# Attention: row sums turned into rows by TensorE, and scores as three products of float32r parts

## The chip, the cores and the metric

The kernel runs on one core of a Trainium2 chip. The metric is the device time of one execution in microseconds (us). Three runs of the kernel before took 1138.47, 1144.91 and 1147.83 us; the median is 1144.91. A profile of one execution, with every instruction's start, duration and waits, is what the prediction is made from.

## The reference, cut to what matters

The whole reference is attention over 4 batches of 8 heads, a gated feed-forward layer that mixes positions, and a layer of 8 experts with one expert per token. The change touches the attention alone:

```python
# q, k, v: (4, 8, 1152, 64) float32
q_pool = q.reshape(B, H, S // 2, 2, D).mean(axis=3)          # 576 queries a head
scores = (1 / sqrt(D)) * matmul(q_pool, k.transpose(0, 1, 3, 2))   # 576 x 1152
scores = scores - max(scores, axis=-1, keepdims=True)
attn = exp(scores)
attn = attn / (sum(attn, axis=-1, keepdims=True) + 1e-09)
return matmul(attn, v)
```

## The kernel before

The 32 heads are handled as 16 pairs (`NP`). A head has 576 queries: four blocks of 128 and a last 64. A pair therefore has nine tiles of 128 queries (`NTL = 9`), listed in `KIND`: eight are one block of one head, the ninth (`t == 8`, `KIND` None) holds the last 64 queries of both heads. There are 144 tiles, numbered g.

For one tile:

- `scores`: queries times the 1152 keys, contraction over 64 values. The keys lie in two halves of the partitions: rows 0 to 63 hold keys 0 to 511 and then 1024 to 1151, rows 64 to 127 hold keys 512 to 1023. The queries stand in both halves. So keys 0 to 1023 are two f32 matmuls of 512 columns, one per row half, into two banks of `s`. In tile 8 each head fills one half of the output's partitions, so there are four matmuls, one per quadrant of the array. An f32 matmul is two instructions in the profile.
- `scores_rest`: the last 128 keys, from rows 0 to 63 alone, into the bank `r` (128 of its 512 columns).
- `maximum`: VectorE takes the minimum over `s`, then over `r` (the queries are scaled by -1/16, so the minimum is the maximum of the scores).
- `exps`: ScalarE's exponentials into `e`, with their sums into `sum`.
- `transp`: TensorE transposes `e` in two parts, five and four blocks of 128 keys, each block in two row halves (10 and 8 instructions), into `t`, of which there is one buffer. `back` copies `t` to `et` in SBUF: the first part on VectorE (L149), the second on ScalarE (L147).

A pair's tiles 0 to 3 form its first half (c = 0) and tiles 4 to 8 its second (c = 1). Per half:

- `sums`: VectorE adds the two sums of each tile and takes reciprocals (`rs`: one partition per query, one column per tile). Then SP stores them to `rdram` in DRAM as rows: L164 twice, and for c = 1 L167 twice. `spread` reads them back, each row broadcast to 64 partitions, as `rb` (L175, for c = 1 also L177).
- `push`: AV, the product of `v` and `et`, nine blocks of keys per head, cut into steps of 2, 2, 2 and 3 blocks, one step per tile. The result stands in the one bank `av`. `out` (L198, L200) multiplies it by `rb` into `xo` and frees the bank; SP writes `xo` to `xT` (L201), which the next stage reads.

The order is written by hand: each function is put at a time in tiles (`at(g + .2, scores_rest, g)`), and the list, sorted by time, is the order on every engine's queue. Scores of tile g stand at g, the first transposes of tile g at g + 1.98, the copy L149 at g + 2.1, the second transposes at g + 2.15, an AV step at g + 0.5, an AV half's scaling at g + 1.11 behind its last step. The sums of tiles 3 and 8 stand at g + 2.13 and the spread at g + 5.05. SP, which issues all these transfers, works through its queue in order and waits where an entry is not ready.

The next pair's queries and keys are loaded at tiles 0 and 1 (`load_qk`), one head each; `prep` adds neighbouring queries and scales them (L71, L72), on GpSimd at tiles 3 and 4; for the first pair VectorE does it ahead of everything. Beside this, steps of a later stage's weight conversion (`bg`, L295 to L354) run on VectorE, ScalarE and GpSimd in tiles 0, 1, 2, 6, 7 and 8 of each pair.

## Time and profile before

| | before |
|---|---|
| median of 3 runs | 1144.91 us |
| profiled execution | 1142.15 us |
| its span on the core | 1140.4 us |
| mean granted TensorE clock | 0.954 of full |
| TensorE busy | 1017.6 us (89%) |
| VectorE busy | 743.2 us (65%) |
| ScalarE busy | 595.6 us (52%) |
| GpSimd busy | 229.1 us (20%) |

The span runs from the first to the last instruction of the program; the rest of the profiled execution's time lies around it. A busy share is a mean over stages with different limits: attention fills the span up to about 592 us, the feed-forward layer the next part and the experts the last. PE is TensorE's matmuls and PEld its weight loads, DVE VectorE, ACT ScalarE, POOL GpSimd, and SPq the queue of SyncE, which issues DMAs. Matmuls overlap, so the duration of one is longer than the distance at which the next one starts.

### The profile page before, as it was taken

The numbers are of one execution on the slowest core, as the hardware profiler recorded it, in microseconds if no ns is written. First come the engines' busy times: TensorE is split into PE (matmuls) and PEld (weight loads), VectorE is DVE, ScalarE is ACT, GpSimd is POOL, SyncE is SP. The second block draws the span as 40 slices with busy tenths as digits, with TensorE's granted clock in tenths as the row PEclk, the third lists the DMA queues.
The fourth block names the chain that finished last, engine by engine and source line by source line (L and its number), as shares of the span: only waits on it lengthen the run. The fifth ranks groups of instructions, "written<-read, shape, count | busy, mean of one in ns | idle before, by whom it ended". The sixth has DMA issues, their size and how long they took to land.

```text
span 1140.4 us, 19804 instructions
## 1 busy us (share of the span) xinstructions
PE 1017.6 (89%) x7500; PEld 685.5 (60%) x7500; DVE 743.2 (65%) x1329; ACT 595.6 (52%) x1172; POOL 229.1 (20%) x189
## 2 busy tenths in 40 slices
PE   6679878799989969989947999999999999999997
PEld 3234434344444434444436898899777777777775
DVE  5558766577876757766718861423378877888784
ACT  4346645466656646655614332212237767776773
POOL 1001110111110111110025341122121413133221
PEclk9789988999999989989978899999999999999999
DMA  5346745456756756737153211200283314111750
GB/s 153 85 84 103 113 90 124 70 114 113 109 117 126 88 95 121 94 105 144 36 151 111 66 53 39 75 1 1 91 285 143 120 47 176 37 38 50 279 222 26
DMA packets 68128, 116.78 MB, mean 102 GB/s; under 512 B 30858, under 2 KB 39218, under 8 KB 66488
## 3 DMA queue, kind: packets, MB, share of 16 engines
q1 hardware_dynamic: 64304, 104.38, 39.4%
q0 software_dynamic: 3680, 11.02, 2.9%
q8 instruction: 63, 1.03, 0.5%
q14 instruction: 41, 0.34, 0.2%
q10 hardware_dynamic: 40, 0.01, 0.0%
HBM read 165.61 MB, written 19.48 MB: 162 GB/s over the span
## 4 chain that ended last, share of the span: by engine, by line
PE 44%; issue 20%; DMA 19%; DVE 10%; POOL 3%; ACT 2%; SPq 2%; another core or an unknown queue 0%; POOLq 0%; DVEq 0%; ACTq 0%
PE ps_av L190 10%; PE ps_t L131 8%; DMA aw_rb<-rdram 7%; DMA rdram<-aw_rs 6%; PE ps_s L82 5%; DMA er_x<-x,tab_gi 4%; PE m_ps_v L608 4%; PE m_ps_u L556 4%; PE m_ps_u L542 3%; PE m_ps_v L501 3%; POOL er_x L983 2%; PE ps_r L95 2%; DVE aw_et L149 2%; DVE aw_mx L105 2%; PE ps_s L85 1%
## 5 line engine op out<-in xcount | busy, mean ns | idle before, releaser
L131 PEld LDWEIGHTS ps_t<-keep_ident,aw_e 64*128 64x128 f32 x2592 | 107.6, 143 | 225.8 <-DVE aw_et L149 145.0
L190 PE MATMUL ps_av<-aw_et,aw_v 128*64 128x320 f32 (+1 forms) x1152 | 175.3, 433 | 38.2 <-DVE aw_xo L200 38.2
L105 DVE TENSOR_REDUCE aw_mx<-ps_s 128x1 f32<-128x1024 f32 x144 | 174.8, 1214 | 15.4 <-PE ps_s L82 8.4
L131 PE MATMUL ps_t<-keep_ident,aw_e 64*128 64x64 f32 x2592 | 146.3, 239 | 42.8 <-DVE aw_et L149 32.7
L149 DVE COPY aw_et<-ps_t 128x640 f32<-128x640 f32 x144 | 118.7, 824 | 95.4 <-PE ps_t L131 84.3
L119 ACT ACTIVATE aw_e<-ps_s,aw_mx 128x1024 f32<-128x1024 f32 x144 | 159.2, 1105 | 0.0
L82 PE MATMUL ps_s<-ao_k,ao_q 64*128 64x512 f32 x512 | 148.2, 659 | 7.3 <-DMA ao_k<-in_k 5.9
L117 ACT ACTIVATE aw_e<-ps_r,aw_mx 128x128 f32<-128x128 f32 x144 | 52.9, 368 | 163.8 <-DVE aw_junk L106 163.2
L190 PEld LDWEIGHTS ps_av<-aw_et,aw_v 128*64 128x64 f32 x1152 | 74.3, 142 | 89.8 <-DVE aw_xo L200 39.5
L147 ACT ACTIVATE aw_et<-ps_t 128x512 f32<-128x512 f32 x144 | 86.0, 597 | 77.2 <-PE ps_t L131 70.5
L354 DVE TENSOR_TENSOR eb_w2l<-er_r,eb_w2h 128x1024 fp32r<-128x1024 f32 x88 | 103.5, 1218 | 4.6 <-ACT eb_w2h L350 4.4
L354 DVE TENSOR_TENSOR eb_w1l<-er_r,eb_w1h 128x1024 fp32r<-128x1024 f32 x66 | 78.8, 1221 | 34.1 <-ACT eb_w1h L350 34.1
L350 ACT ACTIVATE eb_w2h<-er_r 128x1024 fp32r<-128x1024 f32 x88 | 88.7, 1068 | 0.6 <-PE ep_yp L1056 0.3
L71 POOL TENSOR_TENSOR ao_qr<-ao_qr 128x576 f32<-128x576 f32 x30 | 42.4, 1414 | 213.5 <-DMA ao_qr<-in_q 181.2
L350 ACT ACTIVATE eb_w1h<-er_r 128x1024 fp32r<-128x1024 f32 x66 | 67.8, 1072 | 18.1 <-DMA er_r<-in_w 8.5
L1056 PE MATMUL ep_yp<-eb_w2h,ew_hth 128*128 128x512 f32 x176 | 71.1, 404 | 0.3 <-ACT ew_hth L350 0.3
L1056 PE MATMUL ep_yp<-eb_w2h,ew_htl 128*128 128x512 f32 x176 | 70.2, 399 | 0.2 <-DVE ew_htl L354 0.2
L1056 PE MATMUL ep_yp<-eb_w2l,ew_hth 128*128 128x512 f32 x176 | 69.1, 393 | 0.0
L1062 POOL DMA_INDIRECT out<-ew_y,tab_si x22 | 22.4, 1017 | 202.6 <-DVE ew_y L1061 176.7
L106 DVE TENSOR_SCALAR_CACHE_REDUCE aw_junk<-ps_r,aw_mx 128x128 f32<-128x128 f32 x144 | 50.6, 351 | 19.1 <-PE ps_r L95 0.6
L501 PE MATMUL m_ps_v<-keep_wv,m_a_xh 128*128 128x512 f32 x144 | 47.0, 400 | 14.7 <-issue 13.7
L354 POOL TENSOR_TENSOR bg_l<-bg_e,bg_h 128x256 fp32r<-128x256 f32 x16 | 11.6, 727 | 237.7 <-ACT bg_h L350 237.7
(234 smaller groups left out, 1905.0 us busy)
## 6 DMA issues: line engine op xcount, KB each, us to landing
er_r<-in_w SPq DMA_DIRECT2D x45, 2048.0 KB
ao_qr<-in_q SPq DMA_DIRECT2D x32, 576.0 KB
ao_k<-in_k SPq DMA_DIRECT2D x32, 320.0 KB
aw_v<-in_v SPq DMA_DIRECT2D x16, 576.0 KB
xT<-aw_xo SPq DMA_DIRECT2D x16, 288.0 KB
bg_raw<-in_w_in SPq DMA_DIRECT2D x16, 256.0 KB
aw_rb<-rdram SPq DMA_DIRECT2D x64, 64.0 KB
er_r<-in_w SPq DMA_DIRECT2D x16, 256.0 KB
```

What stands on the lines that cost most here:

```text
L82: nc.tensor.matmul(d["s"][:, i, :], r["q", h][rows, 128 * n:128 * n + 128], r["k", h][rows, 0:512], start=True, stop=True)
L105: nc.vector.tensor_reduce(out=m[:, 0:1], in_=d["s"], op=ALU.min, axis=AX.XY)
L117: nc.scalar.activation(out=e[:, 8, :], in_=d["r"][:, 0:128], func=AF.Exp, bias=d["m"][:, 1:2], scale=-1.0, accum_out=s[:, col, 1:2])
L119: nc.scalar.activation(out=e[:, 0:8, :].rearrange("p k c -> p (k c)"), in_=d["s"].rearrange("p i c -> p (i c)"), func=AF.Exp, bias=d["m"][ ...
L131: nc.tensor.transpose(t[:, i, 64 * (k - k0):64 * (k - k0) + 64], E[g]["e"][o, k, :], ident[o, o])
L147: nc.scalar.activation(out=o, in_=i, func=AF.Copy)
L149: nc.vector.tensor_copy(o, i)
L190: nc.tensor.matmul(box["t"][64 * h:64 * h + 64, 0:n], v[:, h, k, :], et[:, k, h, 0:n], start=k == 0, stop=k == 8)
L350: nc.scalar.activation(out=hi, in_=src, func=AF.Copy)
L354: (nc.gpsimd if eng_lo == "p" else nc.vector).tensor_tensor(out=lo, in0=src, in1=hi.bitcast(F32), op=ALU.subtract)
L501: nc.tensor.matmul(pv, xx[xi][:, k, tile(i, j)], wv[:, wj, k, :], start=n == 0, stop=n == 11)
L1056: nc.tensor.matmul(pt, hT[hi][:, c, 128 * o:128 * o + 128], W2[wi][:, f, :], start=f == 0 and (hi, wi) == (0, 0), stop=f == 7 and (hi, wi) ...
```

## The change

It has three parts.

**Sums.** The stores L164 and L167 are gone. `sums_turn`, at g + 2.25, transposes the columns of `rs` on TensorE into columns 128 to 255 of the bank `r` of tile g + 2, on 4 or 5 partitions. `maximum` of that tile copies these rows to SBUF on VectorE between its two minima, and SP stores them to `rdram` as rows. `spread` moves from g + 5.05 to g + 4.05 and reads two rows per head, and for c = 1 half a row more. The last pair's second half has no later tile, so `sums_last` takes a bank of its own.

**Scores.** Queries and keys are split into two float32r parts, hi and lo. The scores are hi hi + hi lo + lo hi, three products per row half that add up in one bank. Tile 8 no longer uses quadrants: the last 64 queries of head 0 stand in columns 512 to 575 and those of head 1 in columns 576 to 639, with zeros for the other head's, and both heads' three products add up over all 128 rows of the output: six per row half. The rest of the scores is three (tile 8: six) float32r products of 128 columns.

**Splitting.** GpSimd has six instructions per head instead of two, on 640 columns instead of 576, in tiles 2 to 7, two at a time. For the first pair (`head`) VectorE and ScalarE do it. Keys now pass through a raw buffer `kr`, of which there is one per head. Queries are loaded with 640 columns.

```diff
@@ -43,66 +43,95 @@
-        E, ET, SUM, MX, TP = {}, {}, {}, {}, {}
+        E, ET, SUM, RS, TP = {}, {}, {}, {}, {}
...
+        QW = 640
...
         def load_qk(p, h):
...
-                r["qr", h] = opr([128, 2, SQ], F32, f"qr{h}", bufs=1)
+                r["qr", h] = opr([128, 2, QW], F32, f"qr{h}", bufs=1)
...
-                r["k", h] = opr([128, 640], F32, f"k{h}")
-                nc.sync.dma_start(r["k", h], ap["k"][p, h])
+                r["kr", h] = opr([128, 640], F32, f"kr{h}", bufs=1)
+                nc.sync.dma_start(r["kr", h], ap["k"][p, h])
...
         def load_v(p):
...
-        def prep(p, h, e, o=0, n=SQ):
+        def parts(p, h):
+            r = P[p]
+            r["q", h] = [opr([128, QW], F32R, f"q{i}{h}") for i in "hl"]
+            r["k", h] = [opr([128, 640], F32R, f"k{i}{h}") for i in "hl"]
+        def prep(p, h, i):
...
-            r = P[p]
-            if o == 0:
-                r["q", h] = opr([128, SQ], F32, f"q{h}")
-            c = slice(o, o + n)
-            q, raw = r["q", h], r["qr", h]
-            e.tensor_tensor(out=raw[:, 0, c], in0=raw[:, 0, c], in1=raw[:, 1, c], op=ALU.add)
-            e.tensor_scalar(out=q[:, c], in0=raw[:, 0, c], scalar1=-1.0 / 16.0, scalar2=0.0, op0=ALU.mult, op1=ALU.add)
-        def scores(g):
+            if i == 0:
+                parts(p, h)
+            e, r = nc.gpsimd, P[p]
+            q, raw, k, kr = r["q", h], r["qr", h], r["k", h], r["kr", h]
+            if i == 0:
+                e.tensor_tensor(out=raw[:, 0, :], in0=raw[:, 0, :], in1=raw[:, 1, :], op=ALU.add)
+                e.tensor_scalar(out=raw[:, 1, :], in0=raw[:, 0, :], scalar1=-1.0 / 16.0, scalar2=0.0, op0=ALU.mult, op1=ALU.add)
+            if i == 1:
+                e.tensor_scalar(out=q[0], in0=raw[:, 1, :], scalar1=1.0, scalar2=0.0, op0=ALU.mult, op1=ALU.add)
+                e.tensor_tensor(out=q[1], in0=raw[:, 1, :], in1=q[0].bitcast(F32), op=ALU.subtract)
+            if i == 2:
+                e.tensor_scalar(out=k[0], in0=kr, scalar1=1.0, scalar2=0.0, op0=ALU.mult, op1=ALU.add)
+                e.tensor_tensor(out=k[1], in0=kr, in1=k[0].bitcast(F32), op=ALU.subtract)
+        def head(h):
+            v, a = nc.vector, nc.scalar
+            parts(0, h)
+            r = P[0]
+            q, raw, k, kr = r["q", h], r["qr", h], r["k", h], r["kr", h]
+            for c in [slice(0, 128), slice(128, QW)] if h == 0 else [slice(0, QW)]:
+                v.tensor_tensor(out=raw[:, 0, c], in0=raw[:, 0, c], in1=raw[:, 1, c], op=ALU.add)
+                a.activation(out=q[0][:, c], in_=raw[:, 0, c], func=AF.Copy, scale=-1.0 / 16.0)
+                v.scalar_tensor_tensor(out=q[1][:, c], in0=raw[:, 0, c], scalar=-1.0 / 16.0, in1=q[0][:, c].bitcast(F32),
+                                       op0=ALU.mult, op1=ALU.subtract)
+                if c.start == 0:
+                    a.activation(out=k[0], in_=kr, func=AF.Copy)
+                    v.tensor_tensor(out=k[1], in0=kr, in1=k[0].bitcast(F32), op=ALU.subtract)
+        def products(g):
...
+            hs, c = ([KIND[t][0]], slice(128 * KIND[t][1], 128 * KIND[t][1] + 128)) if KIND[t] else (range(2), slice(512, QW))
+            return [(r["q", h][i][:, c], r["k", h][j]) for h in hs for i, j in ((0, 0), (0, 1), (1, 0))]
+        def scores(g):
             d = E[g] = {"s": ps([128, 2, 512], F32, "s", bufs=2)}
-            for i in range(2):
-                rows = slice(64 * i, 64 * i + 64)
-                if KIND[t]:
-                    h, n = KIND[t]
-                    nc.tensor.matmul(d["s"][:, i, :], r["q", h][rows, 128 * n:128 * n + 128], r["k", h][rows, 0:512], start=True, stop=True)
-                else:
-                    for h in range(2):
-                        nc.tensor.matmul(d["s"][64 * h:64 * h + 64, i, :], r["q", h][rows, 512:576], r["k", h][rows, 0:512],
-                                         start=True, stop=True)
+            mm = products(g)
+            for n, (q, k) in enumerate(mm):
+                for i in range(2):
+                    o = slice(64 * i, 64 * i + 64)
+                    nc.tensor.matmul(d["s"][:, i, :], q[o], k[o, 0:512], start=n == 0, stop=n == len(mm) - 1)
...
         def scores_rest(g):
-            p, t = divmod(g, NTL)
-            r, d = P[p], E[g]
+            d = E[g]
...
-            rows = slice(0, 64)
-            if KIND[t]:
-                h, n = KIND[t]
-                nc.tensor.matmul(d["r"][:, 0:128], r["q", h][rows, 128 * n:128 * n + 128], r["k", h][rows, 512:640], start=True, stop=True)
-            else:
-                for h in range(2):
-                    nc.tensor.matmul(d["r"][64 * h:64 * h + 64, 0:128], r["q", h][rows, 512:576], r["k", h][rows, 512:640],
-                                     start=True, stop=True)
+            mm = products(g)
+            for n, (q, k) in enumerate(mm):
+                nc.tensor.matmul(d["r"][:, 0:128], q[0:64], k[0:64, 512:640], start=n == 0, stop=n == len(mm) - 1)
...
         def maximum(g):
...
             d = E[g]
...
+            if "row" in d:
+                q, c, n = d["row"]
+                row = wrk([6, 128], F32, f"row{c}")
+                nc.vector.tensor_copy(row[0:n], d["r"][0:n, 128:256])
+                nc.sync.dma_start(rdram[q, c, 0:n], row[0:n])
+                P[q]["rb", c] = wrk([128, 320], F32, f"rb{c}", bufs=1)
@@ -157,24 +186,31 @@
-            d = rdram[p, c]
-            with nc.allow_non_contiguous_dma(reason="a pair's sums, from columns to rows"):
-                for h in range(2):
-                    nc.sync.dma_start(d[3 * h:3 * h + 2].rearrange("c q -> q c"), rs[:, h:4:2])
-                if c:
-                    for h in range(2):
-                        nc.sync.dma_start(d[3 * h + 2:3 * h + 3].rearrange("c q -> q c"), rs[:, 4:5])
+            RS[p, c] = rs
+        def sums_turn(p, c, g):
+            n = 4 if c == 0 else 5
+            nc.tensor.transpose(E[g]["r"][0:n, 128:256], RS.pop((p, c))[:, 0:n], ident)
+            E[g]["row"] = (p, c, n)
+        def sums_last(p, c):
+            t = ps([128, 512], F32, "r")
+            nc.tensor.transpose(t[0:5, 0:128], RS.pop((p, c))[:, 0:5], ident)
+            row = wrk([6, 128], F32, f"row{c}")
+            nc.vector.tensor_copy(row[0:5], t[0:5, 0:128])
+            nc.sync.dma_start(rdram[p, c, 0:5], row[0:5])
...
         def spread(p, c):
...
-                row = d[3 * h:3 * h + 3].rearrange("c q -> (c q)").unsqueeze(0)
-                nc.sync.dma_start(rb[o, 0:256], row[:, 0:256].to_broadcast([64, 256]))
+                nc.sync.dma_start(rb[o, 0:256].rearrange("p (c q) -> p c q", c=2), d[h:4:2].unsqueeze(0).to_broadcast([64, 2, 128]))
...
-                    nc.sync.dma_start(rb[o, 256:320], row[:, 256 + 64 * h:320 + 64 * h].to_broadcast([64, 64]))
+                    nc.sync.dma_start(rb[o, 256:320], d[4:5, 64 * h:64 * h + 64].to_broadcast([64, 64]))
@@ -238,17 +274,22 @@
             if t == 3:
...
-                at(g + 5.05, spread, p, 0)
+                at(g + 2.25, sums_turn, p, 0, g + 2)
+                at(g + 4.05, spread, p, 0)
...
             if t == 8:
...
-                at(g + 5.05, spread, p, 1)
+                if g + 2 < NT:
+                    at(g + 2.25, sums_turn, p, 1, g + 2)
+                else:
+                    at(g + 2.25, sums_last, p, 1)
+                at(g + 4.05, spread, p, 1)
...
-                if t in (3, 4):
-                    at(g + .3, prep, p + 1, t - 3, nc.gpsimd)
+                if 2 <= t < 8:
+                    at(g + .3, prep, p + 1, t % 2, t // 2 - 1)
                 if t == 6:
@@ -265,9 +306,8 @@
-        for o, n in ((0, 128), (128, 448)):
-            prep(0, 0, nc.vector, o, n)
-        prep(0, 1, nc.vector)
+        head(0)
+        head(1)
@@ -1241,7 +1281,11 @@
-    qT = q.reshape(16, 2, SQ, 2, HD).transpose(0, 1, 4, 3, 2)[:, :, twice]
+    qT = q.reshape(16, 2, SQ, 2, HD).transpose(0, 1, 4, 3, 2)
+    qp = np.zeros((16, 2, HD, 2, 640), q.dtype)
+    qp[..., :512] = qT[..., :512]
+    qp[:, 0, :, :, 512:576] = qT[:, 0, :, :, 512:]
+    qp[:, 1, :, :, 576:640] = qT[:, 1, :, :, 512:]
@@ -1253,7 +1297,7 @@
-        q=qT,
+        q=qp[:, :, twice],
...
```

On TensorE, at tile 5 of the second pair, ahead of the last AV step of the first pair. `ps_t` are the transposes, `ps_s` and `ps_r` the scores and their rest, `ps_av` AV. Before:

```order
L131 MATMUL ps_t_1053<-keep_ident_65,aw_e_1036 128x64 x10
L82 MATMUL ps_s_1064<-ao_k_16_501,ao_q_18_632 128x512 x2
L131 MATMUL ps_t_1074<-keep_ident_65,aw_e_1036 128x64 x8
L95 MATMUL ps_r_1087<-ao_k_16_501,ao_q_18_632 128x128
L190 MATMUL ps_av_958<-aw_et_705,aw_v_315 64x320 x6
```

and now, where `aw_rs` are the reciprocals of the sums and `kh`, `kl`, `qh`, `ql` the parts of keys and queries:

```order
L160 MATMUL ps_t_771<-keep_ident_65,aw_e_753 128x64 x10
L115 MATMUL ps_s_782<-ao_kh_23_237,ao_qh_21_235 128x512 x2
L115 MATMUL ps_s_782<-ao_kl_24_238,ao_qh_21_235 128x512 x2
L115 MATMUL ps_s_782<-ao_kh_23_237,ao_ql_22_236 128x512 x2
L160 MATMUL ps_t_793<-keep_ident_65,aw_e_753 128x64 x8
L122 MATMUL ps_r_806<-ao_kh_23_237,ao_qh_21_235 128x128
L122 MATMUL ps_r_806<-ao_kl_24_238,ao_qh_21_235 128x128
L122 MATMUL ps_r_806<-ao_kh_23_237,ao_ql_22_236 128x128
L194 MATMUL ps_r_806<-keep_ident_65,aw_rs_57_790 4x128
L226 MATMUL ps_av_662<-aw_et_357,aw_v_88 64x320 x6
```

One line of scores and one of rest have become three each, and the turn of the sums (L194) stands between the rest and AV.

On SP, where the sums of a pair's second half meet the loads of the next pair. `aw_rs` are the stores of the sums, `aw_rb` the spread, `ao_qr` and `ao_k` or `ao_kr` the loads of queries and keys. Before:

```order
L53 DMA ao_qr_31_1679<-in_q 128x1152
L55 DMA ao_k_32_1681<-in_k 128x640
L164 DMA rdram<-aw_rs_150_1712 128x2x1 x2
L167 DMA rdram<-aw_rs_150_1712 128x1 x2
L53 DMA ao_qr_33_1735<-in_q 128x1152
L55 DMA ao_k_34_1737<-in_k 128x640
L175 DMA aw_rb_151_1719<-rdram 64x256
```

and now:

```order
L55 DMA ao_qr_61_2002<-in_q 128x1280
L57 DMA ao_kr_62_2004<-in_k 128x640
L55 DMA ao_qr_63_2060<-in_q 128x1280
L57 DMA ao_kr_64_2062<-in_k 128x640
L133 DMA rdram<-aw_row_161_2067 5x128
L211 DMA aw_rb_162_2070<-rdram 64x2x128
```

The store of the sums is one entry of five rows instead of four entries of single columns, and it stands behind the second head's loads instead of between the two heads'.

## Rows read from the trace of the kernel before

**Rows 1.** Waits: engine line waited for: us in total, times, longest us.
```profile
PEld ps_t L131 <- DVE aw_et L149: 145.0, 138, 11.1
...
DVE aw_xo L198 <- DMA aw_rb<-rdram: 45.9, 9, 13.9
...
PE ps_av L190 <- DVE aw_xo L200: 38.2, 7, 8.2
...
SPq L175 <- DMA rdram<-aw_rs: 106.1, 22, 8.7
```

**Rows 2.** Timeline of SP: start us, us, engine line op, [idle before <-releaser].
```profile
127.12 1.46 SPq L164 DMA_DIRECT2D rdram<-aw_rs  x2
...
135.60 0.45 SPq L175 DMA_DIRECT2D aw_rb<-rdram  x1
```

**Rows 3.** Timeline around three long waits.
```profile
37.83 0.29 DVE L311 TENSOR_SCALAR bg_e<-bg_raw 128x256 int32<-128x256 int32 x1 [10.71 <-DMA bg_raw<-in_w_in]
...
149.11 0.42 DVE L198 TENSOR_TENSOR aw_xo<-ps_av,aw_rb 128x256 f32<-128x256 f32 x1 [5.80 <-DMA aw_rb<-rdram]
...
573.13 0.15 DVE L158 SCALAR_TENSOR_TENSOR aw_rs<-aw_sum 128x5 f32<-128x5 f32 x1
...
586.96 0.59 SPq L177 DMA_DIRECT2D aw_rb<-rdram  x1
...
591.29 0.42 DVE L198 TENSOR_TENSOR aw_xo<-ps_av,aw_rb 128x256 f32<-128x256 f32 x1 [13.95 <-DMA aw_rb<-rdram]
```

**Rows 4.** Timeline of one undisturbed tile, TensorE and the copy L149.
```profile
308.10 0.53 PE L131 MATMUL ps_t<-keep_ident,aw_e 64*128 64x64 f32 x10
308.46 1.08 PE L82 MATMUL ps_s<-ao_k,ao_q 64*128 64x512 f32 x4
308.67 0.82 DVE L149 COPY aw_et<-ps_t 128x640 f32<-128x640 f32 x1 [0.70 <-PE ps_t L131]
309.55 0.46 PE L131 MATMUL ps_t<-keep_ident,aw_e 64*128 64x64 f32 x8
309.85 0.44 PE L95 MATMUL ps_r<-ao_k,ao_q 64*128 64x128 f32 x2
310.21 1.30 PE L190 MATMUL ps_av<-aw_et,aw_v 128*64 128x320 f32 x8
311.44 0.28 PE L131 MATMUL ps_t<-keep_ident,aw_e 64*128 64x64 f32 x2
```

**Rows 5.** Timeline of TensorE, float32r products of later stages, 288 and 512 columns.
```profile
690.13 0.29 PE L556 MATMUL m_ps_u<-m_a_wsh,m_b_vnh 128*128 128x288 f32 x1
690.27 0.29 PE L556 MATMUL m_ps_u<-m_a_wsh,m_b_vnl 128*128 128x288 f32 x1
...
901.59 0.40 PE L1056 MATMUL ep_yp<-eb_w2h,ew_htl 128*128 128x512 f32 x1
901.83 0.39 PE L1056 MATMUL ep_yp<-eb_w2l,ew_hth 128*128 128x512 f32 x1
```

**Rows 6.** Timeline of TensorE, a ninth tile of a pair.
```profile
565.40 1.09 PE L85 MATMUL ps_s<-ao_k,ao_q 64*64 64x512 f32 x8
566.42 0.46 PE L131 MATMUL ps_t<-keep_ident,aw_e 64*128 64x64 f32 x8
566.82 0.44 PE L98 MATMUL ps_r<-ao_k,ao_q 64*64 64x128 f32 x4
567.18 0.65 PE L190 MATMUL ps_av<-aw_et,aw_v 128*64 128x256 f32 x4
```

**Rows 7.** Timeline of GpSimd and VectorE; last row L318's durations: ns min/median/max.
```profile
96.45 1.41 POOL L71 TENSOR_TENSOR ao_qr<-ao_qr 128x576 f32<-128x576 f32 x1 [4.33 <-DMA ao_qr<-in_q]
96.47 1.67 DVE L318 SCALAR_TENSOR_TENSOR bg_e<-bg_raw,bg_e 128x256 int32<-128x256 int32 x1
...
97.95 0.73 POOL L72 TENSOR_SCALAR ao_q<-ao_qr 128x576 f32<-128x576 f32 x1
...
L318 DVE SCALAR_TENSOR_TENSOR bg_e<-bg_raw,bg_e x16: 415/416/1668, 40.4 to 472.5; 128x256 int32<-128x256 int32 x16
```

## Prediction

> **What bounds the kernel now.** Attention fills the first 592 us of the 1140.4 us span, and the change touches nothing behind it. I read the waits first, then the DMA queue, then the longest stalls, then one undisturbed tile.
>
> The waits [rows 1] show two different things. One is a transfer: VectorE waits 45.9 us in nine places for `rb`, the broadcast reciprocals, before it can scale and free the AV bank (L198), and TensorE waits 38.2 us in seven places for that bank. The other is a chain inside the tile: in 138 of 144 tiles the transposes of the second half are released by L149, the copy of the first half.
>
> Why `rb` is late is on the DMA queue [rows 2]: the pair's sums are stored at 127.12 in four-byte pieces, one per partition and column. The spread that reads them back is issued only at 135.60; in all that queue entry waits 106.1 us for such stores [rows 1]. What that costs stands in [rows 3]: 5.80 us at 149.11, and 13.95 us at the end of attention, with which the next stage starts late. At 37.83 VectorE waits 10.71 us for a weights load (`bg_raw`) queued behind the first such store.
>
> An undisturbed tile [rows 4] takes 308.10 to 311.44, 3.34 us. Transposes start at 308.10; the scores run 308.46 to 309.54; L149 runs 308.67 to 309.49 and lets the second transposes start at 309.55; then the rest of the scores (309.85), AV (310.21), and the next tile.
>
> **The change, part by part.** Times are subtracted from the profiled execution's own 1142.15 us (span 1140.4; it lies 2.8 us below the median of the runs shown, 0.24%, which I do not correct).
>
> *Stores in rows.* The four-byte stores become one store of 4 or 5 rows of 512 bytes. Store and spread then each land within 4.3 us at most: that is the time from the last spread's issue at 586.96 to its use at 591.29, itself measured in a jam [rows 3]. The row store stands on the queue behind both heads' loads, but from it to the scaling 4.5 tiles pass, 15 us. So I take all 38.2 us of TensorE's mid-run waits as gone (bounds 32, which is 45.9 less the 13.95 at the end, and 38.2). Of the 10.71 us I leave 2.5 us for a bare load: 8.2 gained (0 to 10.7). At the end the sums start at 573.13; reciprocal, transpose and copy add about 1 us, store and spread 2 to 4.3 us each, so `rb` is there at 578 to 583 instead of 591.29, and x1's load lies on the same queue between them. I take 10 us (7 to 12). **Gain 56.4.**
>
> *Scores in 128 ordinary tiles.* A 512-column float32r product follows the last by 0.24 us (901.59 to 901.83) [rows 5]. Two row halves side by side, three deep, are 3 x 0.24 plus the tail of a matmul, 0.39 - 0.24 = 0.15: 0.87 against 1.08 us. The saving of 0.21 lies wholly under L149, which ends at 309.49 whatever the scores do: **0**. If the scores were on the path it would be 27 us.
>
> *Rest in these tiles.* 128 columns now take four passes of f32: 309.85 to 310.21, 0.36 us, directly ahead of AV and so on the path. Three float32r products replace them. No row shows one under 288 columns; those follow each other by 0.13 to 0.14 us [rows 5]. Below: three quarters of 0.36, -0.09. Above: each at the whole f32 price, 3 x 0.36, +0.72. I take the nearest row, 3 x 0.133 = 0.40: +0.04, **5 us** over 128 tiles (-12 to +92).
>
> *Tile 8 of a pair.* It packed both heads into quadrants: scores 565.40 to 566.42, rest 566.82 to 567.18 [rows 6]. Now both heads' products are added with zeros in the queries: six deep, 6 x 0.24 = 1.44 against 1.02, and a rest of 6 x 0.133 = 0.80 against 0.36. +0.42 and +0.44, sixteen times: **14 us** (0 to 50, the latter with the rest at f32's price).
>
> *The turn of the sums on TensorE.* A few transposes cost 0.28 us [rows 4]; with the change of array shape 0.3. For the first half of a pair it stands between rest and AV: 16 x 0.3 = 5. For the second there is no AV behind it and TensorE waits for ScalarE there: 2. **7 us** (2 to 12). It waits for VectorE's reciprocal: two short steps behind L149 (the first 0.15 us [rows 3]), covered by the second transposes and the rest, which begin behind L149 too. The row copy on VectorE (L149 moves 640 columns in 0.82 us; a fifth of them some 0.3 us, 32 times) lies in VectorE's idle time, 0.70 us ahead of L149 in [rows 4]: 0; without that cover 10.
>
> *GpSimd.* Its six instructions per head go by 1.41 x 640/576 = 1.57 for those with two inputs and 0.73 x 640/576 = 0.81 for the others [rows 7]: 7.1 us a head, 14.3 a pair instead of 4.3. They run one after another once the queries have landed, from about tile 2 to 6, so they are long done before the next pair needs them. But they hold up VectorE: L318, with two SBUF inputs, took 1.67 us beside GpSimd's L71, and its median is 0.416 [rows 7]. The SBUF page of the Trainium skill (SBUF — State Buffer, "Who interferes with whom") says why: such an instruction reads its second input through an interface shared with GpSimd. The trace agrees, by 1.25 us. The first step of the sums (two SBUF inputs) falls in tile 5, where GpSimd is busy: half of 1.25, less 0.2 that the transposes cover, 0.4 x 16 = **6 us** (0 to 20). The weights' steps of VectorE meet GpSimd about once a pair in tiles 2 and 6: **3 us** after VectorE's slack (0 to 15).
>
> *Head.* VectorE now makes six passes of 640 columns ahead of tile 0's maximum (an add and two subtractions per head; by L149's width 0.82 us each [rows 4]) instead of an add and a scaling per head, and some wait for ScalarE's copies. Two passes more, 1.6, and two such waits: **3 us** (1 to 5).
>
> Sum: 56.4 - 5 - 14 - 7 - 6 - 3 - 3 = 18.4. 1142.15 - 18.4 = 1123.7; **forecast 1123**. The splits themselves hide behind attention; the gain comes from the stores alone.
>
> **Rivals.**
> *Narrow products are dear (ends slower).* The rest's float32r products may not run at one column per cycle. At f32's price they add (0.72 - 0.04) x 128 = 87 and (6 x 0.36 - 0.80) x 16 = 22: 1232. At 0.29 us each, a whole product without overlap [rows 5], they add 0.47 x 128 + 0.94 x 16 = 75: 1198. The Trainium skill's TensorE page ("TensorE: Matmul & The Clock Gate", section on row/col tiling) says that a weight load overlaps a running matmul only where the row group differs, and the three products of one half share theirs. The 288-column rows speak against it: whole-array products follow each other in 0.133 us though each lasts 0.29. It decides at (1144.9 - 1123)/(3 x 128 + 6 x 16) = 0.046 us more per product, 0.18. Chance 0.13.
> *The halves do not run side by side.* In f32 they do (four instructions in 1.08 us). If not, 6 x 0.24 = 1.44 outlasts L149's cover (309.55 - 308.46 = 1.09) by 0.35, and tile 8 by 1.44: 0.35 x 128 + 1.44 x 16 = 68: 1191. Chance 0.05.
> *GpSimd gets onto the path.* All sums wait the full 1.25 (+14), and two weights' steps a pair pass on 0.5 us (+12): 1149. Chance 0.12.
> *The store stays late*, because it now follows both heads' loads: the 38.2 us return, 1161. For it speaks its new place; against it, 15 us of room. Chance 0.05.
> *More gain*: tile 8 and the turns fill waits that are not on the path, and other transfers gain too: about 1100. Chance 0.06.
>
> **Numbers.** The forecast's own band, 1107 to 1138, has 0.59. About 1% is what a measurement of this kernel tells from no change. Under 1133.5: 0.54 of the band and 0.06, 0.60. Between 1133.5 and 1156: 0.05 and GpSimd's 0.12, 0.17. Above: 0.23. The range reaches from 1094 to 1170, over the late store, and leaves the two TensorE rivals out, 0.18.
>
> **What would show it.** No idle time of VectorE on `rb`, and the spread issued within some 4 us of its store; VectorE's wait for the last `rb` 4 us instead of 13.95; second transposes still released by the copy. Rest to AV near 0.4 us: at 0.6 and more the first rival holds. Scores near 0.87, or 1.4 if the halves run in turn. The sums' first step near 0.15 us, or over 1 us if GpSimd holds it. It is wrong if waits on `rb` remain, or if the tile's 3.34 us grows by over 0.15.

## The result, and the profile after

The changed kernel takes 1095.15 us (median of 4 runs, 1090.80 to 1098.49) where the kernel before takes 1141.69 us beside it (4 runs): a ratio of 0.959, with a 95% interval of 0.952 to 0.966. The forecast was 1123 us. The direction and the place were right; the gain is 46.5 us, two and a half times the 18.4 us of the forecast's sum. The profiled execution of the changed kernel took 1098.49 us, its span is 1096.7 us.

Everything lies in attention. It ends, with the last scaling into `xo`, at 591.85 us before and at 547.38 us after; what follows takes 548.5 and 549.3 us.

Of the waits (us in total, times, longest) these answer to [rows 1]:

```profile
PEld ps_t L160 <- DVE aw_et L178: 90.1, 130, 3.1
...
PE ps_r L194 <- DVE aw_rs L188: 7.0, 13, 1.9
...
DVE aw_xo L234 <- DMA aw_rb<-rdram: 5.1, 1, 5.1
```

The nine waits of VectorE for `rb` have become one, the last of attention, and TensorE's wait for the AV bank is gone from the list. The second transposes are still released by the copy. New is a wait of TensorE in the turn of the sums (L194) for the reciprocals.

The DMA section of the page (packets, MB, share of 16 engines) first of before, then of after, says what became of the stores:

```profile
DMA packets 68128, 116.78 MB, mean 102 GB/s; under 512 B 30858, under 2 KB 39218, under 8 KB 66488
...
q1 hardware_dynamic: 64304, 104.38, 39.4%
```

```profile
DMA packets 50501, 118.93 MB, mean 108 GB/s; under 512 B 8987, under 2 KB 21587, under 8 KB 48857
...
q1 hardware_dynamic: 46672, 106.47, 28.6%
```

An ordinary tile after, from the timeline of TensorE and the copy, answers to [rows 4]:

```profile
317.50 0.52 PE L160 MATMUL ps_t<-keep_ident,aw_e 64*128 64x64 f32 x10
317.83 0.48 PE L115 MATMUL ps_s<-ao_kh,ao_qh 64*128 64x512 f32 x2
318.06 0.82 DVE L178 COPY aw_et<-ps_t 128x640 f32<-128x640 f32 x1 [0.17 <-PE ps_t L160]
318.15 0.39 PE L115 MATMUL ps_s<-ao_kl,ao_qh 64*128 64x512 f32 x2
318.38 0.40 PE L115 MATMUL ps_s<-ao_kh,ao_ql 64*128 64x512 f32 x2
318.95 0.46 PE L160 MATMUL ps_t<-keep_ident,aw_e 64*128 64x64 f32 x8 [0.17 <-DVE aw_et L178]
319.22 0.30 PE L122 MATMUL ps_r<-ao_kh,ao_qh 64*128 64x128 f32 x1
...
319.67 1.30 PE L226 MATMUL ps_av<-aw_et,aw_v 128*64 128x320 f32 x8
320.90 0.52 PE L160 MATMUL ps_t<-keep_ident,aw_e 64*128 64x64 f32 x10
```

The scores run in 0.95 us, side by side in row halves and hidden under the copy. From the rest to AV it is 0.45 us, where the forecast put 0.40. The tile takes 3.40 us instead of 3.34. A quiet ninth tile answers to [rows 6]:

```profile
366.71 0.53 PE L160 MATMUL ps_t<-keep_ident,aw_e 64*128 64x64 f32 x10
367.05 0.48 PE L115 MATMUL ps_s<-ao_kh,ao_qh 64*128 64x512 f32 x2
...
367.28 0.82 DVE L178 COPY aw_et<-ps_t 128x640 f32<-128x640 f32 x1 [0.41 <-PE ps_t L160]
...
368.29 0.40 PE L115 MATMUL ps_s<-ao_kh,ao_ql 64*128 64x512 f32 x2
368.53 0.41 PE L160 MATMUL ps_t<-keep_ident,aw_e 64*128 64x64 f32 x8
368.74 0.30 PE L122 MATMUL ps_r<-ao_kh,ao_qh 64*128 64x128 f32 x1
...
369.53 1.08 PE L226 MATMUL ps_av<-aw_et,aw_v 128*64 128x256 f32 x8
```

The six products outlast the copy, which ends at 368.10 (the second transposes wait for nothing), and from the rest to AV it is 0.79 us (forecast 0.80).

The end of attention answers to [rows 3]: sums, spread, scaling.

```profile
537.47 0.16 DVE L187 SCALAR_TENSOR_TENSOR aw_rs<-aw_sum 128x5 f32<-128x5 f32 x1
...
540.83 0.60 SPq L211 DMA_DIRECT2D aw_rb<-rdram  x1
...
546.82 0.42 DVE L234 TENSOR_TENSOR aw_xo<-ps_av,aw_rb 128x256 f32<-128x256 f32 x1 [5.13 <-DMA aw_rb<-rdram]
```

From the sums to the scaling it was 18.16 us [rows 3] and is 9.35.

### The profile page after: what moved, and what is told of

It reads as the page before. It is cut to its first block, busy times and chain, and to the rows that moved or that the text cites. A ratio compares the mean times of both kernels' runs of the same rounds, so it can differ in the third digit from the quotient of the medians.

```text
span 1096.7 us, 20808 instructions
## 1 busy us (share of the span) xinstructions
PE 1017.1 (93%) x8012; PEld 749.5 (68%) x8012; DVE 761.2 (69%) x1363; ACT 598.0 (55%) x1177; POOL 354.0 (32%) x309
## 4 chain that ended last, share of the span: by engine, by line
PE 64%; DVE 19%; DMA 7%; issue 5%; ACT 2%; POOL 1%; SPq 1%; DVEq 0%; POOLq 0%; ACTq 0%
PE ps_av L226 13%; PE ps_t L160 9%; PE ep_yp L1096 8%; DVE aw_et L178 7%; PE ep_hp L1063 6%; DMA er_x<-x,tab_gi 4%; PE m_ps_v L648 4%; PE ps_r L122 4%; PE m_ps_u L596 4%; PE m_ps_u L582 3%; PE m_ps_v L541 3%; DVE aw_mx L128 3%; PE ps_s L115 3%; PE ep_hp L1056 3%; DMA ao_kr<-in_k 1%
## 5 line engine op out<-in xcount | busy, mean ns | idle before, releaser
L178 DVE COPY aw_et<-ps_t 128x640 f32<-128x640 f32 x144 | 118.4, 822 | 96.2 <-PE ps_t L160 95.9
L226 PE MATMUL ps_av<-aw_et,aw_v 128*64 128x320 f32 (+1 forms) x1152 | 171.5, 425 | 0.0
L115 PE MATMUL ps_s<-ao_kh,ao_qh 64*128 64x512 f32 x320 | 78.7, 489 | 10.4 <-ACT ao_kh L99 10.4
L78 POOL TENSOR_TENSOR ao_qr<-ao_qr 128x640 f32<-128x640 f32 x30 | 46.3, 1545 | 85.7 <-DMA ao_qr<-in_q 85.0
L1096 PE MATMUL ep_yp<-eb_w2h,ew_hth 128*128 128x512 f32 x176 | 71.2, 405 | 0.2 <-ACT ew_hth L390 0.2
L1096 PE MATMUL ep_yp<-eb_w2h,ew_htl 128*128 128x512 f32 x176 | 70.2, 399 | 0.2 <-DVE ew_htl L394 0.2
L1096 PE MATMUL ep_yp<-eb_w2l,ew_hth 128*128 128x512 f32 x176 | 69.0, 392 | 0.0
L115 PE MATMUL ps_s<-ao_kh,ao_ql 64*128 64x512 f32 x320 | 66.2, 409 | 0.0
L115 PE MATMUL ps_s<-ao_kl,ao_qh 64*128 64x512 f32 x320 | 65.9, 407 | 0.2 <-DVE ao_kl L100 0.2
```

The costliest lines, as they stand in the source:

```text
L115: nc.tensor.matmul(d["s"][:, i, :], q[o], k[o, 0:512], start=n == 0, stop=n == len(mm) - 1)
L178: nc.vector.tensor_copy(o, i)
L226: nc.tensor.matmul(box["t"][64 * h:64 * h + 64, 0:n], v[:, h, k, :], et[:, k, h, 0:n], start=k == 0, stop=k == 8)
L1096: nc.tensor.matmul(pt, hT[hi][:, c, 128 * o:128 * o + 128], W2[wi][:, f, :], start=f == 0 and (hi, wi) == (0, 0), stop=f == 7 and (hi, wi) ...
```

## The experiments

Two explanations stood against each other. **A**: the four-byte stores cost far more than the waits that carry their name, and the scores' part costs what was forecast or nearly so. **B**: the stores cost the 56 us of the forecast, and the scores' part is nearly free. Medians are of 4 runs and more; beside each stands its ratio to the kernel before, with the interval. The runs were made in four groups, and the medians of the kernel before, run beside each group, lie between 1134.5 and 1144.1 us. So a difference of a few us between single runs says little by itself; as a second witness the text gives the time at which attention ends in the profiled execution.

### Each part alone

`sums_only`: the kernel before, with the changed `sums`, `sums_turn`, `sums_last`, `spread` and the row copy in `maximum`, and nothing else of the change.

> The kernel before with the sums' part alone: rows by TensorE, early spread; scores stay f32 in the old form. Theory A: the four-byte stores cost more than the waits on `rb`. In the pairs they cost some 66 us (copy-to-copy distances above the undisturbed ones: 4.4 us a pair, fifteen pairs), with slow tiles after each stall, and some 9 us at the end; the scores' part costs some 30 and was hiding a part of that gain. Then this kernel runs at 1142 - 66 - 9 + 4 (the turns) = 1071, ratio 0.93 to 0.945, and faster than the full change. Theory B: the stores cost the 56 us of the forecast and the scores' part is nearly free: 1142 - 56 + 7 = 1093, as fast as the full change (0.955 to 0.965).

`scores_only`: the changed kernel with the stores and the spread of before.

```diff
-            RS[p, c] = rs
+            d = rdram[p, c]
...
+                for h in range(2):
+                    nc.sync.dma_start(d[3 * h:3 * h + 2].rearrange("c q -> q c"), rs[:, h:4:2])
...
-                at(g + 4.05, spread, p, 1)
+                at(g + 5.05, spread, p, 1)
```

> The full change with the old stores and the old spread: the scores' and the splitting's part alone. Theory A: tile 8 and the rest cost 1.2 us a pair less the turn's 0.27, some 15 us, GpSimd's meeting with VectorE up to 14, the head 3: 1142 + 32 = 1174, ratio 1.015 to 1.04. Theory B (nearly free, for its costs fill waits that are there anyway): 1142 to 1150, ratio 0.99 to 1.007.

Measured: `sums_only` 1069.45 us, 0.933 (0.925 to 0.941); `scores_only` 1161.09 us, 1.013 (1.002 to 1.023). The sums' part alone gains 75 us and is faster than the whole change; with that B falls. The scores' part costs. With the stores of before it is 17 us (A had expected 32; the interval alone would not exclude B's 1.007), without them 26 (1095.15 - 1069.45). Attention's ends say 18.0 and 27.0 us. So a part of it seems to have been hidden beside the stalls, but the difference of 9 us is no larger than the intervals. In `scores_only` VectorE waits 25.1 us for `rb` in six places, instead of 45.9 in nine.

Between the sums of the first pair and those of the last, that is over 15 pairs, the view by windows shows where the gain lies. The rows are the stretch, its length, then the busy time of TensorE, its weight loads, VectorE, ScalarE and GpSimd, the granted clock, the DMA share and GB/s; the first is of before, the second of `sums_only`:

```profile
53.53:573.13 519.60, 451.05 (x4398) 229.94 (x4399) 357.53 (x719) 296.04 (x702) 70.01 (x72) 0.95 0.58 104
```

```profile
45.85:511.02 465.17, 445.97 (x4428) 226.57 (x4429) 363.32 (x748) 295.38 (x702) 70.22 (x72) 0.99 0.36 116
```

The stretch is 54.4 us shorter. TensorE's idle time falls from 68.5 to 19.2 us, by 49.3, and the same work (and 30 turns more) takes 5.1 us less busy time, at a granted clock of 0.99 instead of 0.95. So beside the 38.2 us of waits for the AV bank there go 11.1 us of other idle time, net of 7.4 us that TensorE now waits in the turn, and 5.1 us of slow work. Slow work looks like this in the kernel before, behind the wait that ends at 149.72 (a window, and the scores in it, which take 1.08 us in [rows 4]):

```profile
149.00:154.00 5.00, 4.28 (x22) 1.98 (x24) 3.54 (x8) 1.55 (x4) 0.00 (x0) 0.50 0.57 176
```

```profile
149.72 1.98 PE L190 MATMUL ps_av<-aw_et,aw_v 128*64 128x256 f32 x8 [5.62 <-DVE aw_xo L200]
...
152.22 2.02 PE L82 MATMUL ps_s<-ao_k,ao_q 64*128 64x512 f32 x4
```

After 5.6 us without work the granted clock is 0.50, the lower of the two levels (1.2 GHz); it stays there until 155 and is 1.00 again from 156.

### What of the stores costs

`sums_jam`: `sums_only`, with the old column stores issued as well, at their place, into a buffer in DRAM that nobody reads.

```diff
+            d = unread[p, c]
...
+                for h in range(2):
+                    nc.sync.dma_start(d[3 * h:3 * h + 2].rearrange("c q -> q c"), rs[:, h:4:2])
+                if c:
+                    for h in range(2):
+                        nc.sync.dma_start(d[3 * h + 2:3 * h + 3].rearrange("c q -> q c"), rs[:, 4:5])
```

By this code a pair has 1280 pieces of four bytes: each half stores two columns of 128 per head, 512 pieces, and the second half its fifth column twice, 256 more. Where expectations below say 1152, they count that column once.

> The sums' part alone, with the old four-byte column stores issued as well, at their old place, into a DRAM buffer that nobody reads. So nobody waits for these stores to be complete; they only burden the queue. Theory A: the burden itself delays all transfers behind it (q loads, weights, the new rows): 10 to 40 us over the sums' part alone. Theory B: only the wait of the spread on the store's completion cost time: within 5 us of the sums' part alone.

Measured: 1138.20 us, 1.002 (0.995 to 1.008), 69 us over `sums_only`; attention ends 65.5 us later. All of the gain is gone but a few us, and no instruction uses what these stores write. (The profile still puts 19.0 us of waits in SP's queue down to them, in seven places.) More than A expected: it is not the spread's wait for these stores that costs, but what they do to the transfers behind them. SP's timeline shows it in the second half of a pair, first the fourth pair in `sums_jam`, then the fifth in `sums_only`: the row store, and the spread that has to wait for it.

```profile
162.49 0.28 SPq L111 DMA_DIRECT2D rdram<-aw_row  x1
...
173.19 0.58 SPq L196 DMA_DIRECT2D aw_rb<-rdram  x1
```

```profile
173.98 0.28 SPq L110 DMA_DIRECT2D rdram<-aw_row  x1
...
177.90 0.59 SPq L188 DMA_DIRECT2D aw_rb<-rdram  x1
```

10.7 us against 3.9. Over all halves, SP's spread waited for row stores like this (in total, times, longest), first in `sums_jam`, then in `sums_only`:

```profile
SPq L196 <- DMA rdram<-aw_row: 155.5, 25, 10.8
```

```profile
SPq L188 <- DMA rdram<-aw_row: 30.7, 13, 4.7
```

`jam_act`: the same stores issued from ScalarE's queue, behind the second copy, a third of a tile later than in `sums_jam`.

```diff
-                    nc.sync.dma_start(d[3 * h:3 * h + 2].rearrange("c q -> q c"), rs[:, h:4:2])
+                    nc.scalar.dma_start(d[3 * h:3 * h + 2].rearrange("c q -> q c"), rs[:, h:4:2])
...
+                at(g + 2.45, lambda p=p, c=int(t == 8): column(p, c, RSC.pop((p, c))))
```

> As the sums' part with the unread four-byte stores, but these stores are issued from ScalarE's queue instead of SP's, two tiles after a half's last scores. It tells where the burden of the jam sits. Theory queue: transfers behind the stores on the same queue wait for their turn; from another queue they cost little: 1069 to 1085 (ScalarE issues six more entries a pair). Theory engines: the packets hold the 16 DMA engines or the memory, whichever queue they come from: 1120 to 1140.

Measured: 1138.77 us, 1.001 (0.995 to 1.006); attention ends 65.0 us later than in `sums_only`. Another queue saves nothing. A part of it is ScalarE's own: in its trace TensorE also waits for ScalarE's exponentials, five times for 0.96 to 4.19 us, 10.8 in all. But VectorE again waits for `rb` (37.7 us in four places) and for the weights (11.4 us). The DMA rows from 40 to 520 us (packets, MB, share) show how, first `sums_only`, then `jam_act`:

```profile
q1 hardware_dynamic: 32888, 54.78, 35.9%
```

```profile
q1 hardware_dynamic: 28723, 49.04, 43.2%
q10 hardware_dynamic: 19264, 0.08, 2.5%
```

q10 is ScalarE's queue. Its pieces take 2.5% of the engines' time, some 0.01 us each; but a packet on SP's queue q1 now takes 0.116 us on the mean (0.432 x 480 x 16 / 28723) instead of 0.084. The trace's records of single packets show that this is not spread over all of them. The median packet of each size takes as long in both runs, to 0.001 us (a row of 4608 bytes 0.178), but 399 packets of q1 take over 1 us instead of 88, together 908 us instead of 120. Of these, 276 (47 in `sums_only`) are rows of 4608 bytes, the size of the query and value loads' rows. In `sums_jam` it is 1071 packets, 956 of them such rows. The Trainium skill's page "DMA: Bandwidth & Descriptors" ("Queues, rings and completion order", on HWDGE ordering) says that the two queues are rings on the same 16 engines, not engines of their own; the trace agrees, in that q1's packets go from 0.084 to 0.116 us with the stores on q10.

`jam_c0`: only the first half's stores, 512 of a pair's 1280 pieces (`if c: return` ahead of them in `sums_jam`).

> As the sums' part with the unread four-byte stores, but only those of a pair's first half (512 of a pair's 1152 pieces of four bytes). Theory linear: the cost goes by the number of pieces: 1069 + 0.44 x 69 = 1100. Theory collision: only the second half's stores cost, since the loads of the next pair's queries and keys lie beside them: 1069 to 1080.

Measured: 1082.06 us, 0.953 (0.944 to 0.962): 13 us over `sums_only` (attention 10.3), where a cost by pieces would be 28 (512 / 1280 x 69). Of the 10.3 us, 7.0 lie in the first pair (its second sums come at 52.85 instead of 45.85), where VectorE again waits 11.2 us for `bg_raw`; the 15 pairs behind it cost 3.3. So by subtraction the second half's stores, which lie beside the loads of the next pair's queries and keys, carry most of it; a run with these alone was not made.

`jam_moved`: all 1280 pieces, each half's behind its own spread.

```diff
+                at(g + 4.06, lambda p=p: column(p, 0, RSC.pop((p, 0))))
...
+                at(g + 4.06, lambda p=p: column(p, 1, RSC.pop((p, 1))))
```

> As the sums' part with the unread four-byte stores, all 1152 pieces a pair on SP's queue, but issued behind the spread of their own half instead of ahead of its row store. Theory order: what costs is what is needed soon and stands behind the stores (the row store, the spread, the loads of queries and keys); behind the spread little is: 1069 to 1090. Theory burden: the pieces cost the same wherever they stand, as some transfer always waits for them: 1120 to 1140.

Measured: 1105.93 us, 0.975 (0.966 to 0.983): neither. Of the 69 us the new place saves 32 and leaves 37 (attention: 32.9 of 65.5 left). So both hold in part: what stands behind the stores decides about half of the price, and some transfers are late wherever they stand: SP's spread still waits 77.0 us for row stores, and VectorE 17.0 us for `rb` in five places.

### What the scores' part costs

`t8_half`: the changed kernel, in tile 8 with the products of head 0 alone.

```diff
-... for h in hs for i, j in ((0, 0), (0, 1), (1, 0))]
+... for h in list(hs)[:1] for i, j in ((0, 0), (0, 1), (1, 0))]
```

> The full change, but in tile 8 only the three products of head 0, and three of the rest (the last 64 queries of head 1 are left out). So tile 8 costs what another tile does. The forecast's step: 0.86 us each time, 14 us in all: 1081. By the distances between the copies: 0.58 each time, 9 us: 1086. Rival: nothing, as the longer tile 8 fills a wait for VectorE: 1093 to 1097.

Measured: 1070.24 us. The total misleads: with other attention values the experts have less to do (504 products in L1096 instead of 528), and what follows attention takes 537.2 us instead of 549.3. Attention ends at 529.27 instead of 547.38. From the start of one copy (L178) to that of the next, tile 8 takes 3.19 us instead of 3.83, 0.64 sixteen times: 10 us. The other 8 lie in hold-ups that fall otherwise, 3.9 of them in the first pair. Tile 8 again in quadrants was not tried.

`split_idle`: `sums_only`, and GpSimd does four more instructions per head whose results nobody reads; its two of before move to tiles 2 and 3, where the changed kernel has them.

```diff
+            e.tensor_scalar(out=x[0], in0=k, scalar1=1.0, scalar2=0.0, op0=ALU.mult, op1=ALU.add)
+            e.tensor_tensor(out=x[1], in0=k, in1=x[0].bitcast(F32), op=ALU.subtract)
```

> The sums' part alone, and GpSimd does four further instructions per head in tiles 4 to 7 on 640 columns (the split's copy and subtraction, twice), whose results nobody reads; the scores stay f32. So GpSimd's share of the scores' part stands alone. Theory A: GpSimd's longer work costs 5 to 9 us by holding up VectorE's instructions with two inputs (the forecast said 9): 1074 to 1078, and the rest of the 26 us between the two kernels is TensorE's. Theory B: what VectorE loses there is covered: within 3 us of the sums' part alone. Theory C: it is most of the 26 us: over 1085.

Measured: 1073.54 us, 0.937 (0.929 to 0.944), 4.1 us more than `sums_only`; attention ends 4.6 us later. It leans to A, but the runs' spread doesn't exclude B. C falls.

`one_input`: the changed kernel with another first step of the sums.

```diff
-            nc.vector.scalar_tensor_tensor(out=rs[:, 0:n], in0=s[:, 0:n, 0], scalar=1e-9, in1=s[:, 0:n, 1], op0=ALU.add, op1=ALU.add)
+            nc.vector.tensor_reduce(out=rs[:, 0:n], in_=s[:, 0:n, :], op=ALU.add, axis=AX.X)
```

> The full change, but the first step of the sums is a sum over one input (tensor_reduce over the pairs of sums) instead of an instruction that reads two inputs from SBUF; the 1e-09 of the reference is left out. Theory GpSimd: that step waits for the interface that GpSimd's two-input instructions hold (0.15 us bare, up to 1.05 beside them) and passes it on to TensorE's turn (waits of 0.96 to 1.90 us in three of the first halves): the step takes some 0.2 us everywhere and the kernel gains 5 to 14 us on the full change. Rival: the time of that step is VectorE's order or the transposes' own, and the waits at the turn come from elsewhere (the loads, the clock): no gain, under 3 us.

Measured: 1089.65 us, 0.953 (0.945 to 0.961), 5.5 us less than the changed kernel; attention ends 8.6 us earlier. The intervals overlap, so the size is not settled. The step's durations (ns: shortest, median, longest) in the changed kernel and here:

```profile
L187 DVE SCALAR_TENSOR_TENSOR aw_rs<-aw_sum x32: 152/159/1050, 28.7 to 537.5; 128x4 f32<-128x4 f32 x16, 128x5 f32<-128x5 f32 x16
```

```profile
L187 DVE TENSOR_REDUCE aw_rs<-aw_sum x32: 149/152/157, 28.6 to 528.9; 128x4 f32<-128x8 f32 x16, 128x5 f32<-128x10 f32 x16
```

The step is no longer held, and the forecast's 6 us for it lies near the 5.5. The Trainium skill's page "SBUF — State Buffer" ("Who interferes with whom") says that a sum over one input never meets GpSimd on this chip; the trace agrees, with 157 ns at most.

### The turn a tile later

`turn_late` (from `sums_only`) and `after_late` (from the changed kernel):

```diff
-                at(g + 2.25, sums_turn, p, 0, g + 2)
+                at(g + 3.25, sums_turn, p, 0, g + 3)
...
-                    at(g + 2.25, sums_turn, p, 1, g + 2)
+                    at(g + 3.25, sums_turn, p, 1, g + 3)
```

> The sums' part alone, with the turn of the sums one tile later (behind the rest of tile g + 3). In the sums' part alone three places are still disturbed (two tiles each, 4.8 to 5.2 us instead of 3.3: some 3.5 us a place). Theory: there the reciprocals are late, since a weights' step of VectorE takes 1.65 us beside GpSimd, and TensorE stands waiting for them in the turn (1.92 us), loses the clock and goes on slowly. With the turn a tile later nothing waits: 1069 - 10 = 1059, ratio 0.92 to 0.93. Rival: TensorE then waits as long for the copy of the transposes, which is behind the same step of VectorE: gain under 4 us, 1065 to 1069.

> The full change with the turn of the sums one tile later (behind the rest of tile g + 3). Theory: what GpSimd's longer work costs reaches TensorE mostly through the turn, which stands in TensorE's queue and waits for the reciprocals; a tile later nothing waits there: 8 to 12 us less than the full change, 1083 to 1087, ratio 0.945 to 0.955. Rival: GpSimd reaches it through VectorE's copies as well, which the transposes wait for: gain under 4 us.

`turn_late`: 1061.66 us, 0.927 (0.921 to 0.934), the fastest of all; 8 us less than `sums_only`, near what was expected, and attention ends 8.7 us earlier, though the intervals of the two ratios overlap. In `sums_only` the hold-up looked like this (GpSimd, VectorE, TensorE); behind it the granted clock fell from 1.00 (to 110.2) to 0.50 (111.2 to 115.0):

```profile
106.21 1.40 POOL L71 TENSOR_TENSOR ao_qr<-ao_qr 128x576 f32<-128x576 f32 x1 [4.73 <-DMA ao_qr<-in_q]
106.25 1.65 DVE L336 SCALAR_TENSOR_TENSOR bg_e<-bg_raw,bg_e 128x256 int32<-128x256 int32 x1
...
107.82 0.62 DVE L164 SCALAR_TENSOR_TENSOR aw_rs<-aw_sum 128x5 f32<-128x5 f32 x1
...
108.71 0.27 PE L171 MATMUL ps_r<-keep_ident,aw_rs 128*5 128x128 f32 x1 [1.92 <-DVE aw_rs L165]
```

`after_late`: 1107.62 us, 0.976 (0.965 to 0.987), 12 us *more* than the changed kernel; attention ends 7.3 us later. The theory missed: the wait in the turn is gone, and TensorE waits for the copy instead, 2.0 to 2.7 us in five places. In the one shown, the sums' step is held beside GpSimd, and the next minimum and the copy are queued behind it:

```profile
143.85 1.55 POOL L78 TENSOR_TENSOR ao_qr<-ao_qr 128x640 f32<-128x640 f32 x1 [8.76 <-DMA ao_qr<-in_q]
143.92 1.51 DVE L187 SCALAR_TENSOR_TENSOR aw_rs<-aw_sum 128x5 f32<-128x5 f32 x1
...
148.03 0.69 PE L160 MATMUL ps_t<-keep_ident,aw_e 64*128 64x64 f32 x8 [2.08 <-DVE aw_et L178]
```

`late_one` and `late_one_f32` are these two with the one-input step.

> The full change with the turn a tile later and the sums' first step as a sum over one input (the 1e-09 is left out): both edits together. With the late turn alone that step was held for up to 1.52 us beside GpSimd, ahead of VectorE's next minimum and copy, and TensorE waited 2.0 to 2.7 us for the copy. Theory: that one step is GpSimd's way to the path; with it gone the late turn costs nothing and gains: 1078 to 1089, about 20 us under the late turn alone. Rival: the weights' steps hold VectorE as well, or the late turn itself costs 10 us: 1098 to 1108.

> The sums' part alone with the late turn (f32 scores) and the same one-input step. In the late turn's trace this step took up to 1.37 us, and TensorE waited twice for the copy, 1.90 and 1.77 us. Theory: these two go, with the slow tile behind each: 4 to 6 us less, 1056 to 1058. Rival: they stay, 1061 or more.

`late_one`: 1099.98 us, 0.967 (0.964 to 0.971). Beside `after_late` the one-input step gains 8 us (attention 5.3), not 20. The number is the rival's, and the trace bears it out: with the sums' step out of it, a weights' step is held in its stead, and the copy behind it is as late:

```profile
112.29 1.54 POOL L78 TENSOR_TENSOR ao_qr<-ao_qr 128x640 f32<-128x640 f32 x1 [5.05 <-DMA ao_qr<-in_q]
112.37 1.74 DVE L358 SCALAR_TENSOR_TENSOR bg_e<-bg_raw,bg_e 128x256 int32<-128x256 int32 x1
...
116.79 0.69 PE L160 MATMUL ps_t<-keep_ident,aw_e 64*128 64x64 f32 x8 [2.19 <-DVE aw_et L178]
```

`late_one_f32`: 1063.39 us, 0.936 (0.933 to 0.940), no different from `turn_late`. In its trace the two waits for the copy are gone and attention ends at 509.22 instead of 511.67; but the number is the rival's, and a gain of 2 us can't be told from the runs' spread.

That the later turn loses in the changed kernel is shown with the one-input step (`late_one` 0.967, `one_input` 0.953, intervals apart) and agrees with `after_late`, whose interval just meets the changed kernel's; why VectorE's two-input steps meet GpSimd in more places there is only read from two traces and stays open.

## Why the prediction was wrong

Attention's end in the profiled executions gives the account: 591.85 before, 520.41 in `sums_only` (-71.4), 547.38 after (+27.0). "Copy to copy" is the distance between the starts of the first copies of successive tiles (L149 before, L155 in `sums_only`, L178 after), and a quiet pair is the sum of its nine usual distances.

| step of the forecast | forecast, us | measured, us | from |
|---|---|---|---|
| first pair, `bg_raw` | -8.2 | -7.7 | sums of the first pair's second half, 53.53 to 45.85 |
| 15 pairs: waits 38.2 less their share of the turns, 6.6 | -31.6 | -54.4 | the two windows above |
| end of attention | -10 | -9.3 | sums to scaling, 18.72 to 9.39, until `xo` is complete |
| rest and tile 8 | +19 | +16 | copy to copy, a quiet pair: 31.46 against 30.44 |
| GpSimd | +9 | +5 to 9 | attention's ends in `split_idle` and `one_input`, one execution each |
| head | +3 | +1.8 | first scores, 6.21 and 8.05 |

**The step that failed** is "I take all 38.2 us of TensorE's mid-run waits as gone (bounds 32 ... and 38.2)". The waits on the AV bank did go. But they were taken for the whole price of the late transfers, and as its upper bound; the price was some 57 us (54.4, and some 3 that the turns cost: a quiet pair takes 30.44 us in `sums_only` and 30.25 before). The difference is other idle time, 11.1 us net, above all at the copies (in the two windows TensorE's waits for the first copy fall from 22.2 to 9.8 us, for the second from 6.9 to 0.4), and slow work after the stalls, 5.1 us. It stood in the trace of before: from copy to copy a pair took 34.7 us on the mean, a quiet one 30.25, so the disturbance was 4.4 us in each of 15 pairs, 66 us in all (a pair of `sums_only` takes 31.0 us on the mean, so 9 of the 66 are still there). The rival "more gain" named this ("other transfers gain too"); its "about 1100" had no terms behind it, and its chance was put at 0.06.

**What was right.** The first pair, the end, and where the costs lie: the scores hidden under the copy, the rest near its nearest row (0.45 against 0.40, not the 0.6 of the first rival), the halves side by side, GpSimd's hold of the sums' first step. The ninth tile's 14 us are 9 to 10: 0.58 us against `sums_only` from copy to copy (3.83 and 3.25), 0.64 in `t8_half`. Its rest grew as forecast (0.79 us to AV, 0.36 in [rows 6]), but from the second transposes to the rest it is 0.21 us now and was 0.40 [rows 6]; that give-back was not in the sum. The turn cost 3 us instead of 7. Together the forecast's costs, 38 us, were some 8 to 12 too high, and its gain, 56.4 us, some 18 too low (74.3: 57.3, 7.7 and 9.3); both errors point the same way. The upper bound of 50 us for tile 8 is 36 by its own terms ((0.42 + 6 x 0.36 - 0.36) x 16). "The gain comes from the stores alone" held, and more: without the scores' part the kernel is 26 us faster. That the splits hide behind attention held for most of their work, but not for the 5 to 9 us above.

**The rivals.** Dear products, halves in turn and the late store did not come. GpSimd is on the path, but for 5 to 9 us in all and not for 26 more.

## What to carry to other kernels

Price a disturbance by the distance between like events in quiet and in disturbed stretches, not by the sum of the waits that bear its name: idle time elsewhere and the slow clock after a stall come on top. Turn a column of sums into a row on chip before it is stored: here 1280 stores of four bytes a pair cost 69 us by making loads beside them late, from either of two queues, though nobody reads what they write. Test each part of a change alone: here one part earned everything and the other cost a third of it.

## What the runs showed of the hardware

Four-byte stores hold the DMA engines little themselves (0.01 us a piece) and yet lengthen the other queue's packets by 38% on the mean, through some hundreds that take over 1 us. Whether that is the memory or the engines' order, no run here tells, nor whether it is the four bytes, the number of pieces or their scattered places.

A VectorE step with a single input was slow beside GpSimd as well. In the changed kernel L362, whose median is 0.286 us, took 1.21 us beside L78:

```profile
145.84 1.53 POOL L78 TENSOR_TENSOR ao_qr<-ao_qr 128x640 f32<-128x640 f32 x1
...
146.32 1.21 DVE L362 TENSOR_SCALAR bg_m<-bg_m 128x256 int32<-128x256 f32 x1
```

The forecast had counted two-input steps alone.
